# Causal attention and a two-branch MoE in one kernel: MoE steps drawn from the first entry whose tokens are there, and shares that count all ready work

## The chip, the cores and the metric

The kernel runs on one core of a Trainium2 chip. Its time is the device time of one execution in microseconds: the median of three runs was 264.66 us (264.55 to 265.04). The profile is of one further execution, which is recorded as 265.55 us; the span from its first to its last instruction is 263.7 us, at a granted TensorE clock of 0.998.

The engines are named as in the profile: PE (TensorE, with PEld for its weight loads), DVE (VectorE), ACT (ScalarE), POOL (GpSimd) and SP (the queue that issues most of the DMAs).

## What is computed

Block-causal attention over 8 batches and 8 heads, 576 tokens of 64 dimensions, followed by a feed-forward layer over all 4608 tokens, with `d_model` 512 and `d_ff` 1024:

```
scores = q @ k.T / 8, kept where query block (64 tokens) >= key block
x      = softmax(scores) @ v, heads side by side   # (4608, 512)
g      = maximum(x @ w1, x @ w2)                   # (4608, 1024)
out    = g @ w_out                                 # (4608, 512)
```

The kernel uses max(h1, h2) = max(h1 - h2, 0) + h2. With d = w1 - w2 and M = w2 @ w_out it computes `out = x @ M + max(x @ d, 0) @ w_out`. So there is one wide product h = x @ d per token, and y adds 4 matmuls against M to 8 against w_out.

## The kernel before

**Attention.** Heads go in pairs (`NPAIR` = 32, a pair's number is p) and pairs in groups of two (`NG` = 16, a group's number is g); two groups make a batch. For a pair, three tiles of scores are made in PSUM (`tile_0`, `tile_1`, `tile_2`), ACT takes their exponentials to `aT` (L391, and a corner at L447), POOL sets masked parts to zero (L396), and two pairs later (`LAG` = 2) `av` multiplies with v (L475). DVE divides by the sum of each row and writes `xp` (L481, L482). The score tiles have two PSUM buffers of two banks each, used by nothing else.

**From xp to xT.** The MoE needs x with features on partitions, as `xT`. For the groups of the first two batches and for the last group `x_out` transposes on PE and copies with DVE or ACT (L513 to L519). For groups 4 to 14 the SP queue transposes by DMA (`x_dma`, L493) after the attention of a group's last pair; for them `x_out` only notes that the tokens of a batch are there. That note is `done_tokens`.

**MoE.** Tokens are cut into ten spans: 256 and 320 of the first batch, then 512 each from token 576 on, the last 448. Spans are not aligned with batches of 576. `h_unit(i, f)` makes one of 8 tiles of h of span i: 4 matmuls, then max with zero by DVE into `g` (L220). With its first tile POOL copies the rows that the last span left over (`carry`, L207). `y_unit(i, s)` makes 128 rows of the output: 12 matmuls into one bank (L257), a copy by ACT (by DVE for the first two spans), and a store by SP (L262, L263). `bT_unit` and `m_unit` make M, at the start. All of these, `av`, the transposes and the warming matmuls share four PSUM banks (`ps_m`). `g` has two buffers.

**The order of the work.** The kernel fixes the order of each engine's instructions itself (`manual_schedule`): instructions stand as they are written. The units are generators that give control back after each matmul. `plan` lists them: for every span h(i, 0) to h(i, 7), and from span 3 on the tiles y(i-1, s) between them. Each entry has the number of tokens that must be there (`need`), a cost per step (1.0 for 512 columns) and its number of steps. `fill(n)` takes steps worth n in that order. It stops where the entry at hand needs tokens that are not there, though a later one may have them: y of span 2 needs 1088 tokens, and stands in the list between tiles of h of span 3, which needs 1600.

**The groups.** The first two groups are written out by hand (L572 to L666), then groups 2 (L667 to L678) and 3 to 15 (L680 to L701). `fill_of(g)` gives the steps of a group: what is `ready`, less 6, over the groups that are left until the next batch is there; the last group takes 45. A group takes them in five fills: `hi` before the first half of each pair's attention, `lo` between its halves, and the rest at the group's end. After the last group come two attentions with fills between them, the last transposes (L709), and all the work that is left (L710).

Of the kernel before, what the change touches and what calls it, by code (L numbers as in the profile page):

```python
# [14 lines left out]
def kernel(  # L15
# [20 lines left out]
    NFF = d_ff // P  # L36
    NTOK = B * S
# [109 lines left out]
    for j in range(d_ff // WB):  # L147
        row, n = (1, j) if j < 3 else (3, 0)
# [50 lines left out]
    done_tokens = [0]  # L199
# [82 lines left out]
    units = []  # L282
    NY = NDM + NFF

    def plan():
        def h(i, f):
            t0, w = spans[i]
            units.append((h_unit(i, f), t0 + w, w / SPAN, NDM))

        def y(i, s, last=False):  # L290
            t0, w = spans[i]
            if last:
                units.append((y_last(i, s), t0 + w, 0.333, 3 * NY))
            else:
                units.append((y_unit(i, s), t0 + w, 1.0, NY))

        for i in range(NSPAN):
            for f in range(NFF):
                h(i, f)
                if i == 0 and f % 2:  # L300
                    units.append((bT_unit(f // 2), 0, 0.25, 2 * NDM))
                if i > 2 and f % 2 == 0 and f // 2 < tiles[i - 1]:
                    y(i - 1, f // 2)
            if i == 1:
                for n in range(2 * NDM):
                    units.append((m_unit(n // NDM, n % NDM), 0, 0.5, NFF))
                for j in range(2):
                    for s in range(tiles[j]):
                        y(j, s)
        n = tiles[-1]  # L310
        for s in range(n):
            y(NSPAN - 1, s, s == n - 1)

    plan()
    steps = [(u, need, cost) for u, need, cost, n in units for _ in range(n)]
    at = [0]


    def ready():
        n, total = at[0], 0.0  # L320
        while n < len(steps) and steps[n][1] <= done_tokens[0]:
            total += steps[n][2]
            n += 1
        return int(total)

    def fill(n):
        while n > 0 and at[0] < len(steps) and steps[at[0]][1] <= done_tokens[0]:
            u, _, cost = steps[at[0]]
            next(u)
            n -= cost  # L330
            at[0] += 1


    def warm_up(n):
# [38 lines left out]
    def pad_keys(p):  # L373
        nc.gpsimd.tensor_copy(
            out=kz_r[p % NT].rearrange("p (a c) -> p a c", c=BLK)[:, 0:3:2],
            in_=kT_r[p % NT][:, S - 3 * BLK:].rearrange("p (a c) -> p a c", c=BLK)[:, 0:3:2],
        )
# [50 lines left out]
    def tile_0(p):  # L428
        u = ps_s.tile([P, 2, 512], FP32, name="ps_s", tag="s")
        scores(p, u, 0, 0, 0, 512)  # L430
        return lambda: (exp(p, u, 512, 0), mask(p, 0))

    def tile_1(p):
        u = ps_s.tile([P, 2, 512], FP32, name="ps_s", tag="s")
        scores(p, u, 0, 0, 512, 64)
        scores(p, u, 64, 1, 128, 448)
        return lambda: (exp(p, u, 512, 512), mask(p, 576))

    def tile_2(p):
        u = ps_s.tile([P, 2, 512], FP32, name="ps_s", tag="s")  # L440
        corner_scores(p, u, 320)
        scores(p, u, 0, 2, 256, 320)
        scores(p, u, 384, 3, 448, P)

        def out():
            exp(p, u, 512, 1024)
            nc.scalar.activation(  # L447
                out=aT_r[p % NA][BLK:, :, 1536:AW], in_=u[BLK:, :, 320:320 + BLK],
                func=AF.Exp, scale=scale,
            )  # L450
            mask(p, 1024)
            mask(p, 1344)
        return out

    def region(*tiles):
        for out in tiles:
            out()
# [29 lines left out]
    def x_by_dma(g):  # L487
        return BY_DMA <= g < NG - 1

    def x_dma(g):  # L490
        b, u = divmod(g, GPB)
        for s in range(2):
            nc.sync.dma_start_transpose(  # L493
                out=xT[:, 2 * u + s, b * S:b * S + NCH * P].rearrange(
                    "p (t w) -> p t w", w=P),
                in_=xps[g][:, s].rearrange("p t a d -> p (t a d)"),
            )

    def x_out(g, t0=0, t1=NCH, copies=(dve, dve)):
        b, u = divmod(g, GPB)  # L500
        if x_by_dma(g):
            if u == GPB - 1:
                done_tokens[0] = (b + 1) * S
            return
        xp = xps[g]
        n = t1 - t0
        n_odd = min(t1, NCH - 1) - t0
        pe = ps_m.tile([P, 2, n, BLK], BF16, name="ps_xe", tag="m")
        po = ps_m.tile([P, 2, n_odd, BLK], BF16, name="ps_xo", tag="m")
        for s in range(2):  # L510
            for t in range(t0, t1):
                src = xp[:, s, t].rearrange("p a d -> p (a d)")
                nc.tensor.transpose(pe[:, s, t - t0, :], src[:BLK], ident[:BLK, :BLK])  # L513
                if t < NCH - 1:
                    nc.tensor.transpose(po[:, s, t - t0, :], src[BLK:], ident[BLK:, BLK:])
        dst = xT[:, 2 * u:2 * u + 2, b * S + t0 * P:b * S + t1 * P].rearrange(
            "p s (t h w) -> p s t h w", h=2, w=BLK)
        copies[0](out=dst[:, :, :, 0], in_=pe[:])
        copies[1](out=dst[:, :, :n_odd, 1], in_=po[:])  # L519
        if u == GPB - 1:  # L520
            done_tokens[0] = min(b * S + t1 * P, (b + 1) * S)
# [8 lines left out]
    def fill_of(g):  # L530
        if g == NG - 1:
            return 45
        left = 5 - g if g < 5 else 2 - (g - 5) % 2
        return -(-max(0, ready() - KEEP) // left)


    def pool_work(s):
        g, i = divmod(s, 2)
        if s == 4:
            load_qk(4, (SP, SP), gated=True)  # L540
        elif s == 5:
            load_qk(5, (SP, SP), gated=True)
            cast("q", 4, ((pool, 0, RPP),))
            cast("k", 4, ((pool, 0, RPP),))
        else:
            if i == 1 and g + 3 < NG:
                load_qk(g + 3, (SP, SP), gated=True)
            if i == 1 and g + 2 < NG:
                cast("q", g + 2, ((pool, 0, RPP),))
                cast("k", g + 2, ((pool, 0, RPP),))  # L550
            nb, j = divmod(s + 2, HP)
            if nb < B:
                for c in ((0, 1), (2, 3), (4,), ())[j]:
                    load_v(nb, c)
# [4 lines left out]
    def t_pair(s):  # L559
        outs = [transposes(nm, g, (dve, act)) for nm, g in T_AT.get(s, [])]  # L560
        return lambda: [f() for f in outs]
# [5 lines left out]
    def av_with(p, n):  # L567
        av(p, [0, 1])
        fill(n)
        av(p, [2, 3, 4])  # L570
# [55 lines left out]
    masks_q(1)  # L626
    load_w(3)
    fill(4)
    burst_q1(2)
    transposes("q", 2, (dve, act))()  # L630
# [18 lines left out]
    load_qk(3, (SP, SP), gated=True)  # L649
    x_out(0, 2, NCH)  # L650
    fill(2)
    diff_w(1)
    outs = tile_0(4), tile_1(4)
# [15 lines left out]
    n = fill_of(GPB)  # L669
# [9 lines left out]

    for g in range(GPB + 1, NG):  # L680
        a, b = 2 * g, 2 * g + 1
        if x_due:
            x_out(x_due.pop())
        n = fill_of(g)
        region(tile_0(a), tile_1(a))
        lo, hi = max(3, n // 18), n * 2 // 9
        for p, tiles in ((a, lambda: (tile_2(a), tile_0(b))), (b, lambda: (tile_1(b), tile_2(b)))):
            fill(hi)
            av_with(p - LAG, lo)
            if p % 2 and x_by_dma(g - 1):  # L690
                x_dma(g - 1)
            copy_out = t_pair(p)
            outs = tiles()
            copy_out()
            region(*outs)
            if p % 2 and g + 1 < NG:
                pad_keys(p + 1)
                pad_keys(p + 2)
            pool_work(p)
        x_due.append(g - 1)  # L700
        fill(n - 2 * (lo + hi))  # L701
    for p in range(NPAIR - LAG, NPAIR):
        if x_due:
            x_out(x_due.pop())
        av_with(p, 5)
        if p % 2 and x_by_dma(p // 2):
            x_dma(p // 2)
        fill(9)
    x_out(NG - 1)  # L709
    fill(len(steps))  # L710

# [33 lines left out]
```

The softmax here doesn't subtract the row's maximum and nothing guards it: scores larger than these inputs give would overflow.

## Time and profile before

| engine | busy us | share of the span | instructions |
|---|---|---|---|
| PE, matmuls | 250.0 | 95% | 2983 |
| PEld, weight loads | 139.6 | 53% | 2983 |
| DVE | 137.2 | 52% | 301 |
| ACT | 140.9 | 53% | 198 |
| POOL | 109.9 | 42% | 274 |

How to read the views. A line of a timeline has start, duration, engine, line of the kernel, operation, output and inputs, the count, and in brackets the idle time of the engine just before it and what ended that. A line of waits has the waiting engine and line, then whom it waited for, then the sum in us, the number of times and the longest. A table of stretches has, for each stretch, its length and then the busy time of PE, PEld, DVE, ACT and POOL with the number of instructions in brackets, the granted clock, the mean share of the DMA engines and GB/s. [...]

The groups are found in PE's timeline by their first score matmuls: group 5 begins at 67.93 us, group 8 at 100.26, group 9 at 113.32. For groups 6 and 7 the point is taken where PE came to these matmuls, 75.85 and 85.05 us; both then waited 0.32 us. The last transposes of xp on PE begin at 213.13 us.

### The profile page before, as it was taken

The numbers are of one execution on the slowest core, as the hardware profiler recorded it, in microseconds if no ns is written. First come the engines' busy times: TensorE is split into PE (matmuls) and PEld (weight loads), VectorE is DVE, ScalarE is ACT, GpSimd is POOL, SyncE is SP. The second block draws the span as 40 slices with busy tenths as digits, with TensorE's granted clock in tenths as the row PEclk, the third lists the DMA queues.
The fourth block names the chain that finished last, engine by engine and source line by source line (L and its number), as shares of the span: only waits on it lengthen the run. The fifth ranks groups of instructions, "written<-read, shape, count | busy, mean of one in ns | idle before, by whom it ended". The sixth has DMA issues, their size and how long they took to land.

```text
span 263.7 us, 7204 instructions
## 1 busy us (share of the span) xinstructions
PE 250.0 (95%) x2983; PEld 139.6 (53%) x2983; DVE 137.2 (52%) x301; ACT 140.9 (53%) x198; POOL 109.9 (42%) x274
## 2 busy tenths in 40 slices
PE   8698799999989799999999999999999999999995
PEld 2346566856546455555555555555555544444444
DVE  4867996656668554545454545454544452323200
ACT  2788552676797484848575757575755100111111
POOL 2987914484577647254635563456311000000000
PEclk9999999999999999999999999999999999999999
DMA  7999996689599949986997599679613411112122
GB/s 247 314 218 298 188 234 158 247 94 252 144 182 256 234 68 264 132 252 71 262 150 232 81 227 178 227 82 126 106 42 81 52 66 57 63 58 82 40 95 104
DMA packets 71265, 41.30 MB, mean 157 GB/s; under 512 B 53568, under 2 KB 58048, under 8 KB 71232
## 3 DMA queue, kind: packets, MB, share of 16 engines
q1 hardware_dynamic: 28544, 31.27, 43.2%
q0 software_dynamic: 42272, 8.92, 38.1%
q10 hardware_dynamic: 416, 0.66, 0.7%
q8 instruction: 23, 0.38, 0.6%
q14 instruction: 10, 0.08, 0.1%
HBM read 34.60 MB, written 9.44 MB: 167 GB/s over the span
## 4 chain that ended last, share of the span: by engine, by line
PE 85%; DMA 5%; POOL 3%; ACT 2%; DVE 2%; issue 1%; ACTq 0%; POOLq 0%
PE ps_y L257 35%; PE ps_h L215 21%; PE ps_o L475 10%; PE ps_s L367 7%; PE ps_w L337 3%; DMA qraw<-in_q_dram 3%; PE ps_M L238 3%; PE ps_qT L348 2%; ACT aT L391 2%; DMA xT<-xp 2%; PE ps_kT L348 2%; POOL vv L136 1%; PE ps_y L272 1%; PE ps_s L385 1%; POOL wo_sb L168 1%
## 5 line engine op out<-in xcount | busy, mean ns | idle before, releaser
L391 ACT ACTIVATE aT<-ps_s 128x1024 bf16<-128x1024 f32 (+2 forms) x100 | 95.9, 996 | 28.9 <-PE ps_s L367 26.9
L220 DVE TENSOR_SCALAR g<-ps_h 128x512 bf16<-128x512 f32 (+3 forms) x80 | 50.7, 636 | 63.9 <-PE ps_h L215 62.9
L215 PE MATMUL ps_h<-xT,d_sb 128*128 128x512 bf16 (+3 forms) x320 | 71.7, 358 | 1.8 <-DVE d_sb L162 1.2
L257 PE MATMUL ps_y<-wo_sb,g 128*128 128x512 bf16 x280 | 69.9, 379 | 0.0
L396 POOL MEMSET aT<- 64x128 bf16 x124 | 22.3, 200 | 78.7 <-ACT aT L391 78.0
L475 PEld LDWEIGHTS <-aT 128*128 128x128 bf16 x960 | 37.2, 98 | 14.0 <-issue 2.1
L215 PEld LDWEIGHTS <-d_sb 128*128 128x128 bf16 x320 | 28.7, 98 | 29.7 <-issue 3.5
L262 ACT COPY y<-ps_y 128x512 f32<-128x512 f32 x31 | 18.2, 588 | 48.5 <-PE ps_y L257 45.6
L257 PEld LDWEIGHTS <-g 128*128 128x128 bf16 x280 | 25.7, 98 | 30.0 <-issue 2.6
L475 PE MATMUL ps_o<-vv,aT 128*128 128x65 bf16 x960 | 39.7, 194 | 0.0
L257 PE MATMUL ps_y<-m_sb,xT 128*128 128x512 bf16 x140 | 37.9, 380 | 0.0
L367 PE MATMUL ps_s<-qT,kT 64*128 64x64 bf16 (+6 forms) x344 | 31.4, 280 | 3.9 <-ACT aT L447 1.6
L136 POOL DMA_DIRECT2D vv<-in_v_dram x40 | 33.7, 848 | 1.6 <-issue 1.2
L482 DVE TENSOR_TENSOR xp<-ps_o,rec 128x256 bf16<-128x256 f32 (+1 forms) x64 | 31.4, 491 | 2.2
L481 DVE RECIPROCAL rec<-ps_o 128x4 f32<-128x4 f32 (+1 forms) x64 | 12.1, 189 | 35.4 <-PE ps_o L475 34.9
L356 ACT COPY qT<-ps_qT 128x576 bf16<-128x576 bf16 (+1 forms) x17 | 10.3, 614 | 24.8 <-PE ps_qT L348 24.8
L257 PEld LDWEIGHTS <-xT 128*128 128x128 bf16 x140 | 12.9, 98 | 16.0 <-issue 3.0
L132 POOL CAST qn<-qraw 128x1152 bf16<-128x1152 f32 (+1 forms) x16 | 16.9, 1058 | 8.6 <-DMA qraw<-in_q_dram 8.6
L367 PEld LDWEIGHTS <-kT 64*128 64x128 bf16 x344 | 12.3, 94 | 13.7 <-issue 8.2
L207 POOL COPY g<-g 128x512 bf16<-128x512 bf16 x8 | 4.9, 613 | 31.5 <-DVE g L220 30.9
L132 POOL CAST kn<-kraw 128x1152 bf16<-128x1152 f32 (+1 forms) x15 | 17.1, 1139 | 1.1 <-DMA kraw<-in_k_dram 1.0
L356 ACT COPY kT<-ps_kT 128x576 bf16<-128x576 bf16 x15 | 9.6, 639 | 10.5 <-PE ps_kT L348 10.0
(57 smaller groups left out, 161.8 us busy)
## 6 DMA issues: line engine op xcount, KB each, us to landing
qraw<-in_q_dram SPq DMA_DIRECT2D x16, 576.0 KB, 4.8
out_dram<-y SPq DMA_DIRECT2D x35, 256.0 KB, 2.6
kraw<-in_k_dram SPq DMA_DIRECT2D x15, 576.0 KB, 6.0
vv<-in_v_dram POOLq DMA_DIRECT2D x32, 128.0 KB, 6.0
w1raw<-in_moe_w_dram POOLq DMA_DIRECT2D x4, 512.0 KB, 7.8
xT<-in_moe_w_dram POOLq DMA_DIRECT2D x4, 256.0 KB, 8.5
wo_sb<-in_moe_w_out_dram POOLq DMA_DIRECT2D x2, 512.0 KB, 8.1
kraw<-in_k_dram ACTq DMA_DIRECT2D x1, 576.0 KB, 5.6
```

The lines of the kernel that those rows point to most:

```text
L132: copy(out=n[:, j0:j1], in_=t[:, j0:j1])
L136: nc.gpsimd.dma_start(out=vv_r[b % NV][P - rows:, c, :, :D], in_=v[b, :, c * P:c * P + rows, :].rearrange("h p d -> p h d"),)
L215: nc.tensor.matmul(pt[:, :w], d_sb[:, c, f * P:(f + 1) * P], xT[:, c, t0:t0 + w], start=(c == 0), stop=(c == NDM - 1),)
L220: nc.vector.tensor_scalar_max(g[:, f, m:m + w], pt[:, :w], 0.0)
L257: nc.tensor.matmul(py[:], lhs, rhs, start=(n == 0), stop=(n == len(terms) - 1),)
L262: (dve if i < 2 else act)(out=y[:], in_=py[:])
L356: (copy or copies[i])(out=t[:, p0 * RPP:p1 * RPP].rearrange("q (p j) -> q p j", j=RPP), in_=pts[i][:, :, p0:p1].rearrange("q j p -> q p j"),)
L367: nc.tensor.matmul(ps[:, hh, col:col + w], kT[r, k0:k0 + P], qT[r, q0:q0 + w], start=True, stop=True,)
L391: nc.scalar.activation(out=aT_r[p % NA][:, :, a0:a0 + w], in_=ps[:, :, :w], func=AF.Exp, scale=scale,)
L396: (eng or nc.gpsimd).memset(aT_r[p % NA][BLK:, :, a0:a0 + BLK], 0.0)
L475: nc.tensor.matmul(po[:, gi, hh, :], a[:, hh, a0:a0 + P], vv[:, c, h0 + 2 * hh, :], start=(mm == 0), stop=(mm == n_mm - 1),)
L482: nc.vector.tensor_mul(xp[:, :, ts[0]:ts[0] + n, p % 2].rearrange("q s t d -> q t s d"), po[:, :, :, :D], rec[:, :n].to_broadcast([P, n, 2 ...
```

## The change

The list of steps becomes a list of units, `todo`, with one unit in hand, `current`. `fill` finishes the unit in hand, and then takes the first one in the list whose tokens are there, whatever stands before it. It returns what it could not spend. `ready` adds up all units whose tokens are there. In groups whose newest tokens come by DMA, the first fill sees the tokens of before first, and what it can't spend so goes to the new ones. At the end, 12 steps of old work stand after the last transposes before the new tokens count.

```diff
-    steps = [(u, need, cost) for u, need, cost, n in units for _ in range(n)]
-    at = [0]
+    todo = [[n, u, need, cost] for u, need, cost, n in units]
+    current = []
     def ready():
-        n, total = at[0], 0.0
-        while n < len(steps) and steps[n][1] <= done_tokens[0]:
-            total += steps[n][2]
-            n += 1
-        return int(total)
+        return int(sum(n * cost for n, _, need, cost in current + todo if need <= done_tokens[0]))
     def fill(n):
-        while n > 0 and at[0] < len(steps) and steps[at[0]][1] <= done_tokens[0]:
-            u, _, cost = steps[at[0]]
-            next(u)
-            n -= cost
-            at[0] += 1
+        while n > 0:
+            if not current:
+                k = next((k for k, t in enumerate(todo) if t[2] <= done_tokens[0]), None)
+                if k is None:
+                    return max(0, n)
+                current.append(todo.pop(k))
+            t = current[0]
+            next(t[1])
+            n -= t[3]
+            t[0] -= 1
+            if not t[0]:
+                current.pop()
+        return 0
...
     for g in range(GPB + 1, NG):
         a, b = 2 * g, 2 * g + 1
+        old = done_tokens[0]
         if x_due:
             x_out(x_due.pop())
-        n = fill_of(g)
+        n, new = fill_of(g), done_tokens[0]
...
-            fill(hi)
+            if p == a and x_by_dma(g - 2):
+                done_tokens[0] = old
+            rest = fill(hi)
+            done_tokens[0] = new
+            fill(rest)
             av_with(p - LAG, lo)
...
+    old = done_tokens[0]
     x_out(NG - 1)
-    fill(len(steps))
+    done_tokens[0] = old
+    fill(NY)
+    done_tokens[0] = NTOK
+    fill(len(units) * NFF * 12)
```

## The prediction

> **What bounds the kernel now.** I read the page first (shares, slices), then the waits of TensorE in two stretches, then PE's timeline group by group, and last the DMA transposes.
>
> ```profile
> PE 250.0 (95%) x2983; PEld 139.6 (53%) x2983; DVE 137.2 (52%) x301; ACT 140.9 (53%) x198; POOL 109.9 (42%) x274
> PE   8698799999989799999999999999999999999995
> PE 85%; DMA 5%; POOL 3%; ACT 2%; DVE 2%; issue 1%; ACTq 0%; POOLq 0%
> ```
>
> TensorE is the bound: 95% of the span, 85% of the chain that ended last. It is not full everywhere: after the opening, slices 12 and 13 (6.6 us each, so 72.5 to 85.7 us) fall to 8 and 7. The waits of TensorE between 66 and 92 us:
>
> ```profile
> PE ps_s L367 <- ACT aT L447: 1.6, 2, 0.8
> PE ps_s L367 <- DVE g L220: 0.6, 2, 0.3
> PE ps_h L215 <- DMA xT<-xp: 0.5, 1, 0.5
> ```
>
> The same question from 92 us to the end lists no wait at all. So from there only the number of matmuls counts, and a matmul moved forward out of that stretch shortens it by a whole matmul. Busy times by stretch, cut at the first score matmul of groups 5, 6, 7 (the third only to its q transposes), then everything after, then two later groups (8 and 9):
>
> ```profile
> core 0: us, PE busy (x) PEld busy (x) DVE busy (x) ACT busy (x) POOL busy (x), PEclk, DMA share, GB/s
> 67.93:75.85 7.92, 7.92 (x154) 4.94 (x147) 6.48 (x15) 6.10 (x8) 4.66 (x13) 1.00 0.71 217
> 75.85:85.05 9.20, 8.06 (x140) 4.86 (x141) 6.38 (x15) 7.56 (x11) 7.59 (x19) 1.00 1.47 219
> 85.05:91.20 6.15, 4.43 (x50) 2.33 (x49) 2.90 (x6) 3.40 (x5) 4.28 (x12) 1.00 1.38 187
> 91.20:260.60 169.40, 169.40 (x1752) 89.17 (x1749) 74.21 (x152) 82.56 (x118) 52.95 (x138) 1.00 0.66 126
> 100.26:113.32 13.06, 13.06 (x167) 7.07 (x166) 6.65 (x14) 8.62 (x12) 6.59 (x18) 1.00 1.18 186
> 113.32:126.37 13.05, 13.05 (x166) 7.04 (x166) 6.67 (x14) 8.62 (x12) 6.63 (x18) 1.00 0.87 173
> ```
>
> To be seen: group 6 lasts 9.20 us with PE busy 8.06; the start of group 7 lasts 6.15 with 4.43; later groups last 13.05 without a gap. ACT is busy 7.56 of 9.20 us in group 6, so there the exponentials set the pace. PE's timeline shows where it stands:
>
> ```profile
> 76.17 0.39 PE L367 MATMUL ps_s<-qT,kT 64*128 64x512 bf16 x2 [0.32 <-DVE g L220]
> 77.39 0.39 PE L367 MATMUL ps_s<-qT,kT 64*128 64x64 bf16 x4 [0.82 <-ACT aT L447]
> ...
> 85.37 0.39 PE L367 MATMUL ps_s<-qT,kT 64*128 64x512 bf16 x2 [0.32 <-DVE g L220]
> 86.59 0.40 PE L367 MATMUL ps_s<-qT,kT 64*128 64x64 bf16 x4 [0.82 <-ACT aT L447]
> 86.91 1.90 PE L215 MATMUL ps_h<-xT,d_sb 128*128 128x512 bf16 x8
> 88.65 0.34 PE L475 MATMUL ps_o<-vv,aT 128*128 128x65 bf16 x6
> 89.46 0.86 PE L215 MATMUL ps_h<-xT,d_sb 128*128 128x512 bf16 x2 [0.47 <-DMA xT<-xp]
> ```
>
> A group's first scores come before the exponentials of the last group's tiles have left the two score buffers, and h of span 3 comes before its tokens are transposed. Both happen because these groups carry too little MoE work in between.
>
> **What the Trainium skill says.** "TensorE: Matmul & The Clock Gate", section "Wait — 56ns, not 53.3ns?", gives 215.7 ns from start to start for 512 columns. The trace agrees; the chain that ended last has
>
> ```profile
> 202.09 2.59 PE ps_y L257 x12
> ```
>
> which is 215.8 ns each, while the rows of such matmuls show 379 ns, because they overlap. I cost a matmul at 0.2158, not at its row. "Perfetto Trace Analysis", section "Tensor Engine Instruction (MATMUL, LD_WEIGHTS)", says that the end of a matmul is an estimate. That agrees too: the gaps listed are shorter than the time lost (below). "DMA: Bandwidth & Descriptors", section "Issuing engines are not separate DMA queues", says that transfers from all engines interleave on the same 16. Here one transpose took 3.1 to 7.0 us to land, depending on what else was under way.
>
> **The change, part by part.** The unit of account is one `fill` step, one matmul of 512 columns. I followed `fill`, `ready` and `fill_of` through the span list (256, 320, eight spans from token 576, the last of 448).
>
> 1. *Up to the end of group 4: nothing.* No work is passed over there; the counts and their order are the same (32, 31 and 30 steps for groups 2 to 4).
>
> 2. *Shares of groups 5 and 6.* With 1152 tokens there, the old count stops at the first h of span 3 (needs 1600): 38 ready, so (38-6)/2 = 16 steps for each group. The new count adds y of span 2 (needs 1088), 4x12 = 48 steps: 86 ready, 40 steps each, all of which it finds. So 2x24 = 48 matmuls move from the tail (245 steps after the last attention in the old, 12+185 = 197 in the new) into groups 5 and 6. From group 7 on both have 40 a group, and 45 in the last.
>
> 3. *What they cost in groups 5 and 6.* A full group lasts 13.055 us (mean of the two rows above) with 40 steps: 40x0.2158 = 8.63, so 4.42 us are scores, transposes and attention. A group with 16 steps would last 4.42+3.45 = 7.87 without a wait. Measured: group 5 7.92 (0.05 over), group 6 9.20 (1.33 over), start of group 7 6.15 against 3.99 in groups 8 and 9 (100.26 to 104.25; 113.32 to 117.31): 2.16 over. Together 3.54 us lost. The gaps recorded make (9.20-8.06)+(6.15-4.43) = 2.86; as ends are estimates, I take 3.54 and keep 2.86 as the lower end.
>
> 4. *What takes the place of the waits.* With 18 steps (3.9 us) before the next group's scores, in place of 4 (0.86 us), the last exponentials (1.95+0.27 us) are out, as they are in groups 8 to 14. The transposes of group 6 land 5.3 us after issue; h of span 3 reaches them 15.5 us after the group's first score (115.78-100.26), the issue is at 9.2 (109.41-100.26), so 1.1 us are to spare. Then all 3.54 us go.
>
> 5. *h of span 2 starts in the first fill of group 5*, after six y matmuls. Its tokens come from DVE copies that end at 69.0 us (68.18+0.49, then 0.41), and PE gets there at 68.5+6x0.2158 = 69.8. No wait.
>
> 6. *Order in the later groups.* Old: every group finishes 4 h and 2 y tiles. New: odd groups finish 8 h and 1 y, even groups 3 y. DVE in odd groups: 6.65+4x0.69 = 9.4 of 13.06 us; ACT in even groups: 8.62+0.59 = 9.2. Both stay under PE. Inside a run of h a tile takes PE 0.86 us and DVE 0.69. The tightest reuses of the four shared PSUM banks, by the built order: y's bank taken by q's transposes 0.99 us after y's last matmul (ACT starts about 0.2 later and takes 0.59); and y's bank of an odd group's first fill taken by attention at 3.1 us after the group's start, while ACT, behind two exponentials, frees it at 2.9 (103.16-100.26). The old order has its own reuse at 0.99 us, h by DVE, in nine places and shows no wait. I take zero, and keep 0.1 us in ten groups, 1 us, as the upper end.
>
> 7. *POOL's copy of g's carry (0.61 us) and g's two buffers.* The copy is issued with h's first step as before, but the h that it reads has been done for a whole group, not for a moment; POOL, behind it masks and casts, can only gain. y of the span before is complete when h starts, so no buffer is missing. Zero, hidden under PE.
>
> 8. *SP.* The y stores move: an even group's third y is now ready at about 12.4 us into the group, when the two transposes are issued (9.2 to 12.5) and the next q and k loads stand ahead of it in the queue. It starts as the transposes land (114.4 to 115.2 in group 8). Zero; up to 0.7 us at each of five boundaries kept for the rival.
>
> 9. *Tokens withheld in the first fill of odd groups.* h of the new span comes after 6 old steps before and after (h before, y now). Zero. In the tail too h of span 8 comes 13 matmuls after the last transposes in both. Zero.
>
> Sum: -3.54 us on a traced span of 263.7, that is 260.2; that execution counts as 265.55 in the times. On the median of 264.66: **261.1 us**.
>
> **Rivals.**
> - *A: part is given back.* The new order waits where a bank, ACT or a transpose is just late (items 6 and 8): 1 us from banks, or 0.5 us at three boundaries. Against it: no wait at all in 169 us of the same machinery. Gain 1.5 to 2.8: 262.5 us.
> - *B: slower, by late transposes.* If even groups, now with one store more, saw the landing of the most crowded group (issue at 148.57 us: 7.0 and 6.1 us), the second transpose would land at 10.5+6.1 = 16.6 us, and h needs it at 15.7 (the fourth h step). 0.87 us at the starts of groups 7, 9, 11, 13 and 15 make 4.4: 261.1+4.4 = 265.5 us. It decides against the change from 0.71 us each (3.54/5). Against it: that was an odd group, with four v loads; even groups have one, and landed in 3.0 to 5.3.
> - *C: nothing moves.* A tail as long as before would need TensorE waiting in the tail by 10.4 us (48x0.2158) or in groups 5 and 6 as much; it is excluded for the tail, where every y evacuation (0.59) hides under 2.59 us of matmuls. Waits of half a microsecond in each of seven groups give 264.6 us.
>
> **How the numbers follow.** Main case 0.78, its own range 260.6 to 261.9 (lower end: 0.5 us more, from small gaps that the rows hide; upper: the recorded 2.86). A 0.13, B 0.05, C 0.04. A change under 0.2% (0.5 us) can't be told from none. Faster: main and A, 0.91; same: C, 0.04; slower: B, 0.05. The range 260.3 to 262.7 takes in the main case and A's likelier part.
>
> **What would show it.** Right: groups 5 and 6 last about 13 us each; TensorE has no wait on ACT's L447 form or on a transpose from group 5 on; group 7's first score comes about 9.0 us later (26.1 for 17.1), and from it to the end is about 12.5 us less (10.36 of matmuls and 2.16 of waits). Wrong: new waits of attention or q transposes for ACT's y copy, h waiting for transposed tokens at the start of odd groups, or groups over 13.1 us.

## The result, and the profile after

| | time, us | against before |
|---|---|---|
| before | 264.68 median (264.55 to 265.04, 4 runs) | 1 |
| changed | 261.19 median (260.83 to 261.69, 4 runs) | 0.9867, 95% interval 0.9847 to 0.9887 |
| changed, again, in a later set | 261.20 median (260.65 to 261.56, 6 runs) | 0.9843 (0.9819 to 0.9867) |

261.1 us was predicted, from a median before of 264.66. In the later set the kernel before has a median of 265.09 us. Ratios and intervals, here and below, leave out two runs in a slower state of the chip, one of the kernel before (268.08 us, granted clock 0.987) and one of experiment 7 (269.04 us, 0.986).

The page of the changed kernel's profile, its first line and PE's row of slices (now 6.5 us each):

```profile
PE 244.8 (94%) x2949; PEld 139.4 (54%) x2983; DVE 137.6 (53%) x301; ACT 141.3 (55%) x198; POOL 109.8 (42%) x274
PE   8688799999999999999999999999999999999995
```

The two slices with 8 and 7 are gone; the slices under 9 that are left are the first five, ahead of the change, and the last one, as before. The count of matmuls is 2949 for 2983 weight loads: 34 records are missing in this trace. That matters for the waits of TensorE from 66 to 260 us, where the list has only these:

```profile
PE ps_h L215 <- issue: 1.0, 6, 0.2
PE ps_y L257 <- issue: 0.8, 5, 0.2
```

They wait for nothing that the profile shows, and those that I followed in the timeline stand where a fill shows one matmul less than it issues (7 where 8 are). In the trace of the second run of the same kernel this view lists nothing at all. The waits for `aT`, for DVE and for a DMA transpose are gone. Groups 5 to 8, in the table of stretches (length, then busy time of PE, PEld, DVE, ACT, POOL):

```profile
67.41:80.44 13.03, 12.77 (x175) 7.17 (x171) 10.31 (x21) 7.55 (x10) 7.59 (x22) 1.00 0.85 168
80.44:93.44 13.00, 12.79 (x165) 7.08 (x166) 4.42 (x11) 9.31 (x13) 6.59 (x18) 1.00 1.08 191
93.44:106.43 12.99, 12.78 (x163) 7.08 (x166) 8.87 (x18) 8.03 (x11) 6.62 (x18) 1.00 0.99 168
106.43:119.42 12.99, 12.78 (x163) 7.07 (x165) 4.41 (x11) 9.31 (x13) 6.57 (x18) 1.00 1.01 195
```

To be seen: groups 5 and 6 now last as long as the later ones. DVE carries the odd groups (busy 10.31 and 8.87 us) and ACT the even ones (9.31); neither gets near 13. PE's timeline has the scores of groups 6 and 7, and h of span 3, at once:

```profile
80.44 0.61 PE L371 MATMUL ps_s<-qT,kT 64*128 64x512 bf16 x6
93.44 0.61 PE L371 MATMUL ps_s<-qT,kT 64*128 64x512 bf16 x6
...
95.28 0.59 PE L215 MATMUL ps_h<-xT,d_sb 128*128 128x512 bf16 x2
95.89 0.81 PE L215 MATMUL ps_h<-xT,d_sb 128*128 128x512 bf16 x3
```

The brackets with idle time that stood on the same matmuls before are missing. The two traces by stretch, cut at the same points as in the prediction (group 15 starts at 191.65 us before and 197.53 after):

| stretch | before | after | difference | predicted |
|---|---|---|---|---|
| start to group 5 | 67.93 | 67.41 | -0.52 | 0 |
| groups 5 and 6 | 17.12 | 26.03 | +8.91 | +9.0 |
| group 7 | 15.21 | 12.99 | -2.22 | -2.16 |
| groups 8 to 14 | 91.39 | 91.10 | -0.29 | 0 |
| group 15 to the end | 72.05 | 61.67 | -10.38 | -10.36 |
| span | 263.7 | 259.2 | -4.5 | -3.54 |

The first row is not the change: up to there the program is the same, and in the traces of the experiments group 5 starts anywhere from 67.25 to 68.14 us. The rest is -3.98 us, 0.44 more than predicted. Of this, 0.29 us lie in groups 8 to 14, where I had set zero. Those groups do not all last the same: five take 12.99 or 13.00 us, group 9 takes 13.02 and group 10 13.11, where before each took 13.05 or 13.06. Group 10 holds a wait that is new:

```profile
132.44:145.55 13.11, 12.90 (x164) 7.16 (x166) 4.42 (x11) 9.31 (x13) 6.60 (x18) 1.00 1.07 191
134.90 0.60 PE L257 MATMUL ps_y<-wo_sb,g 128*128 128x512 bf16 x2
135.86 0.59 ACT L262 COPY y<-ps_y 128x512 f32<-128x512 f32 x1 [0.98 <-ACT aT L395]
136.37 0.55 PE L352 MATMUL ps_qT<-ident,qn 64*128 64x64 bf16 x18
```

The last matmul of y starts at 135.12, ACT copies its bank from 135.86 to 136.45, and of the 18 transposes of q the first starts at 136.37 and the second, which waits for ACT, only at 136.50. In group 8 ACT starts its copy 0.46 us after the start of y's last matmul, here 0.74, and there the first two transposes start within 0.01 us of each other. So q's transposes wait 0.12 us for y's bank, without a bracket in the timeline. The second trace of the same kernel and that of experiment 6 have it too (group 10 lasts 13.11 and 13.10 us). Why ACT starts later in this one group is open.

The experiments ask two things: where the 0.06 us in most of these groups comes from, and, the larger question, whether the reason for the 3.5 us is the right one.

The theory: TensorE lost 3.5 us because groups 5 and 6 had too few steps between a group's last exponentials and the next group's scores; 48 steps brought forward from a tail without gaps fill that time. The rivals: the order of drawing as such, the holding back of new tokens, or merely the place where the steps stand inside a group.

### The profile page after: what moved, and what is told of

Read it like the earlier page. It is cut to its first block, busy times and chain, and to the rows that moved or that the text cites. A ratio compares the mean times of both kernels' runs of the same rounds, so it can differ in the third digit from the quotient of the medians.

```text
span 259.2 us, 7161 instructions
## 1 busy us (share of the span) xinstructions
PE 244.8 (94%) x2949; PEld 139.4 (54%) x2983; DVE 137.6 (53%) x301; ACT 141.3 (55%) x198; POOL 109.8 (42%) x274
## 4 chain that ended last, share of the span: by engine, by line
PE 85%; DMA 5%; POOL 3%; issue 2%; ACT 2%; DVE 1%; POOLq 0%; ACTq 0%
PE ps_y L257 35%; PE ps_h L215 22%; PE ps_o L479 10%; PE ps_s L371 8%; DMA qraw<-in_q_dram 5%; PE ps_M L238 3%; PE ps_qT L352 2%; PE ps_kT L352 2%; POOL vv L136 1%; ACT aT L395 1%; PE ps_y L272 1%; DVE qn L132 1%; PE ps_w L341 1%; PE ps_s L389 1%; POOL wo_sb L168 1%
## 5 line engine op out<-in xcount | busy, mean ns | idle before, releaser
L215 PE MATMUL ps_h<-xT,d_sb 128*128 128x512 bf16 (+3 forms) x306 | 67.4, 357 | 2.7 <-DVE d_sb L162 1.2
L257 PE MATMUL ps_y<-wo_sb,g 128*128 128x512 bf16 x275 | 69.1, 379 | 0.4 <-issue 0.3
L257 PE MATMUL ps_y<-m_sb,xT 128*128 128x512 bf16 x128 | 36.5, 380 | 1.2 <-issue 0.8
L257 PEld LDWEIGHTS <-xT 128*128 128x128 bf16 x140 | 12.2, 98 | 15.1 <-issue 3.5
```

Source lines behind the costliest of these rows:

```text
L215: nc.tensor.matmul(pt[:, :w], d_sb[:, c, f * P:(f + 1) * P], xT[:, c, t0:t0 + w], start=(c == 0), stop=(c == NDM - 1),)
L257: nc.tensor.matmul(py[:], lhs, rhs, start=(n == 0), stop=(n == len(terms) - 1),)
```

## The experiments

**1. The order alone.** The changed kernel, with the old way of counting:

```diff
-        return int(sum(n * cost for n, _, need, cost in current + todo if need <= done_tokens[0]))
+        total = 0.0
+        for n, _, need, cost in current + todo:
+            if need > done_tokens[0]:
+                break
+            total += n * cost
+        return int(total)
```

> The new order of drawing with the old counting: ready stops at the first entry in the list whose tokens are not there, so groups 5 and 6 get 16 steps again, not 40. Theory (the gain is the 48 matmuls that the shares move): the waits of the score matmuls at the start of groups 6 and 7 are back, about 1.3 us each; only the wait for the DMA transpose at the start of group 7 is gone (0.65 us), since y of span 2 now stands ahead of h of span 3. 264.0 us (263.5 to 264.6). Rival (the gain comes from the order itself, fewer hand-overs between h and y): 261.2 to 262.5 us.

Measured 264.0 us, as expected, ratio 0.9972 (0.9960 to 0.9983). Waits of TensorE from 66 to 260 us in its trace:

```profile
PE ps_s L376 <- ACT aT L456: 1.6, 2, 0.8
PE ps_s L376 <- DVE g L220: 0.6, 2, 0.3
```

These are the two score waits of the kernel before, to the tenth; the wait for the transpose is gone. The order is worth 0.3%, the shares the other 1.0 to 1.3%. From the first score of group 5 to that of group 15 this trace takes 122.64 us, against 123.72 before: 1.08 less. Of this, 0.90 us lie in group 7, and the rest in groups 9, 11 and 13, which last 12.99 us.

**2. The slack by itself.** The kernel before, with matmuls of zeros in the two groups and nothing moved:

```diff
             fill(hi)
+            if g in (5, 6):
+                warm_up(5)
...
         fill(n - 2 * (lo + hi))
+        if g in (5, 6):
+            warm_up(14)
```

> The kernel before with 24 more matmuls of zeros, 512 columns, in each of groups 5 and 6 (5 after each hi fill, 14 at the group's end), whose results nothing reads; no MoE work is moved. It prices the slack alone. Theory: 48 x 0.2158 = 10.36 us of matmuls, of which 3.5 us lie in waits that vanish: 264.7 + 6.8 = 271.5 us (271.0 to 272.2). Rival (the slack is only the recorded 2.86 us): 272.2. Rival (no slack, the gain of the change came from elsewhere): 275.0 us.

Measured 271.97 us against 264.87, ratio 1.0268 (1.0243 to 1.0292). So 10.36 us of matmuls cost 7.1 us (6.4 to 7.7 by the interval), and 3.3 us (2.6 to 3.9) of them lay in waits. That interval holds both 3.54 and 2.86, so the time alone can't choose between the two; it does exclude "no slack" (275.0 us). The trace is sharper. Its score matmuls of groups 6 and 8:

```profile
80.42 0.61 PE L367 MATMUL ps_s<-qT,kT 64*128 64x512 bf16 x6
...
106.41 0.61 PE L367 MATMUL ps_s<-qT,kT 64*128 64x512 bf16 x6
```

From group 5 (67.39) to group 8 are 39.02 us, against 32.33 before: 6.69 more for 10.36 us of matmuls, so 3.67 us lay in waits, by one trace against one. Its trace lists no wait of TensorE after 66 us. The recorded idle time alone (2.86) is below what the trace has.

**3. Half of the steps.** The tail gives up 48 steps as in the changed kernel, but only 24 of them go to groups 5 and 6. The count of ready work then hands the other 24 to groups 7 and 8, which take 52 steps each.

```diff
+        if g in (5, 6):
+            return 28
         left = 5 - g if g < 5 else 2 - (g - 5) % 2
```

> The changed kernel with the shares of groups 5 and 6 fixed at 28 steps, not 40: half of the 48 matmuls are moved into them, the others go to groups 7 and 8, which have no wait to fill. Theory (steps pay only until the waits are filled; 10 steps, 2.16 us, now stand between the last tiles of a group and the next scores, against 2.2 us of exponentials): nearly the whole gain, 261.2 to 261.9 us, with at most 0.4 us of waits at the start of groups 6 and 7. Rival (gain in proportion to the steps moved): 262.9 us.

Measured 261.54 us, ratio 0.9877 (0.9855 to 0.9900): 24 steps in groups 5 and 6 bring practically what 48 bring. Groups 5 and 6 last 10.44 and 10.50 us, within 0.05 of 4.42 us of other work plus 28 x 0.2158, and the only wait in the list is another one, in group 7:

```profile
PE ps_h L215 <- ACT y L262: 0.2, 1, 0.2
```

Group 7 lasts 16.04 us, 0.40 more than 4.42 plus 52 x 0.2158; that is about what this run is slower than the changed kernel. A step pays only while a wait is left to fill. After that it costs in the group what it saves in the tail. The table of stretches can't say where that point is; this run shows that 28 steps are enough, and none was made between 16 and 28.

**4. The small remainder.** The kernel before, with one engine changed for the copies of y:

```diff
-                (dve if i < 2 else act)(out=y[:], in_=py[:])
+                dve(out=y[:], in_=py[:])
```

> The kernel before with all copies of y out of PSUM made by DVE, not ACT. It tests a small second source: groups 8 to 14 last 13.055 us before and 12.99 after, and in the trace of before the first matmul of a y tile starts 0.08 us late, just after ACT, behind two exponentials, has freed a bank. Theory (that bank wait is the 0.06 us): groups 8 to 14 fall to about 12.99 us, 264.2 us in all. Rival (the 0.06 us is the price of more hand-overs between h and y): 13.055 us as before and 264.7 us.

Measured 264.58 us, ratio 0.9991 (0.9978 to 1.0004): no difference in the time that these runs can tell, where 264.2 us was expected. The interval holds a gain of 0.4 us as well as none, so the time decides nothing. The groups say which theory holds. In PE's timeline of this kernel the scores of groups 8 and 9 start at

```profile
100.32 0.61 PE L367 MATMUL ps_s<-qT,kT 64*128 64x512 bf16 x6
113.32 0.61 PE L367 MATMUL ps_s<-qT,kT 64*128 64x512 bf16 x6
```

and every group from 8 to 14 lasts 12.99 to 13.01 us, where before it was 13.055, with every hand-over between h and y in its place. So the 0.06 us was y's bank, freed late by ACT. In the timeline of before, the matmul that then waited, and the ACT copy that freed its bank:

```profile
102.71 0.60 PE L215 MATMUL ps_h<-xT,d_sb 128*128 128x512 bf16 x2
103.22 0.38 PE L257 MATMUL ps_y<-m_sb,xT 128*128 128x512 bf16 x1
...
102.57 0.59 ACT L262 COPY y<-ps_y 128x512 f32<-128x512 f32 x1
```

Two steps from 102.71 end at 103.14; the next starts at 103.22, just after 103.16. No idle time is written beside it, because the row of the matmul before still covers it. With DVE's copies the same matmul follows at once (two steps from 102.78, the next at 103.21). In the one execution that was traced (265.12 us, a slower one of this kernel), the gain of these groups was lost in group 7, where the wait for the transpose is 1.3 us and not 0.5:

```profile
PE ps_h L215 <- DMA xT<-xp: 1.3, 2, 1.1
```

Whether DVE's copies make that wait longer is open. They are not needed for it: in the next experiment, where ACT copies, the same wait is 1.3 us too. The transposes meant took 4.5 and 5.3 us to land in the trace of before, 5.2 and 6.0 here.

**5. Full groups, but the later ones go short.** The kernel before, old `fill`, with span 2's y tiles listed right after its h tiles, so that groups 5 and 6 take 40 steps:

```diff
-                if i > 2 and f % 2 == 0 and f // 2 < tiles[i - 1]:
+                if i > 3 and f % 2 == 0 and f // 2 < tiles[i - 1]:
                     y(i - 1, f // 2)
+            if i == 2:
+                for s in range(tiles[2]):
+                    y(2, s)
```

> The kernel before, old fill and old counting, with one edit to the list: y of span 2 stands right after h of span 2, so groups 5 and 6 find 86 steps and take 40 each, as in the changed kernel. Later y tiles stay between tiles of the next h, out of reach, so groups 7 and 8 now find 38 and take 16 each. Theory (the step that counts is that work in reach never runs short again, not the fuller groups 5 and 6 alone): the waits turn up two groups later, at the starts of groups 8 and 9, about 3.5 us in all, and the time is that of before, 264.3 to 265.2 us. Rival (full groups 5 and 6 are enough, later groups have slack of their own): 261.2 to 262.0 us.

Measured 265.13 us against 265.09, ratio 0.9998 (0.9983 to 1.0012). All the idle time of TensorE from 66 to 125 us in its timeline:

```profile
101.87 0.39 PE L370 MATMUL ps_s<-qT,kT 64*128 64x512 bf16 x2 [0.32 <-DVE g L220]
103.08 0.39 PE L370 MATMUL ps_s<-qT,kT 64*128 64x64 bf16 x4 [0.82 <-ACT aT L450]
111.07 0.39 PE L370 MATMUL ps_s<-qT,kT 64*128 64x512 bf16 x2 [0.32 <-DVE g L220]
112.28 0.40 PE L370 MATMUL ps_s<-qT,kT 64*128 64x64 bf16 x4 [0.82 <-ACT aT L450]
115.20 0.38 PE L215 MATMUL ps_h<-xT,d_sb 128*128 128x512 bf16 x1 [0.50 <-DMA xT<-xp]
116.41 0.38 PE L215 MATMUL ps_h<-xT,d_sb 128*128 128x512 bf16 x1 [0.83 <-DMA xT<-xp]
```

The same score waits with the same lengths, two groups later (group 8 comes to its scores at 101.5 us, group 9 at 110.8), and a wait for transposes that is longer (1.33 us for 0.47). Groups 5 and 6 are full and nothing is gained. The rule "first entry whose tokens are there" matters because it keeps every later y in reach, not because it fills these two groups.

**6. No tokens held back.**

```diff
-            if p == a and x_by_dma(g - 2):
-                done_tokens[0] = old
-            rest = fill(hi)
-            done_tokens[0] = new
-            fill(rest)
+            fill(hi)
...
-    done_tokens[0] = old
-    fill(NY)
-    done_tokens[0] = NTOK
```

> The changed kernel without holding back new tokens: no old tokens in the first fill of odd groups, and after the last transposes no 12 steps of old work. In the groups this alters nothing, since six steps of y in hand come first anyway. In the tail h of span 8 comes after 1 step, 0.2 us, while its tokens leave PSUM by DVE about 1.3 us after the first transpose. Theory: one new wait of 0.7 us in the tail, 261.9 us. Rival (the holding back of tokens is part of the gain in the groups, by sparing waits for DMA transposes): 263 us or more. Rival (DVE is early enough): 261.2 us.

The edit leaves the order of matmuls in the groups as it is, since there six steps of y in hand come first with it and without it. Only the tail differs.

Measured 261.29 us, ratio 0.9859 (0.9835 to 0.9883), with 261.20 for the changed kernel in the same set: no difference. The only wait that the list has, after 66 us, with the copy that ended it:

```profile
219.53 0.59 PE L215 MATMUL ps_h<-xT,d_sb 128*128 128x512 bf16 x2
219.82 0.41 DVE L523 COPY xT<-ps_xo 128x512 bf16<-128x512 bf16 x1
220.29 2.54 PE L215 MATMUL ps_h<-xT,d_sb 128*128 128x512 bf16 x11 [0.16 <-DVE xT L523]
```

I expected 0.7 us. The first two h matmuls read the rows of group 14, which were there long before; only the third reads the last group's. From 219.53 two steps end at 219.96, and the third starts at 220.29: 0.33 us. Holding tokens back costs nothing and is worth no more than that here.

**7. The same 16 steps in another place.** The kernel before, groups 5 and 6 with 12 steps at the end and 1 in each earlier fill:

```diff
         lo, hi = max(3, n // 18), n * 2 // 9
+        if g in (5, 6):
+            lo, hi = 1, 1
```

> The kernel before with the 16 steps of groups 5 and 6 kept, but 12 of them at the group's end and 1 in each earlier fill. It asks if the waits at the starts of groups 6 and 7 come of where the steps stand or of how many there are. Theory (too few steps: ACT needs 7.6 us of exponentials and copies in a group of 7.9 us of PE work, so a wait taken away at one place comes back at another): the waits at the group starts vanish and new ones of about 0.5 to 1 us stand inside the groups, before the second pair of tiles; 264.0 to 265.2 us. Rival (placement alone): 262.0 to 263.0 us.

Measured 265.59 us, ratio 1.0017 (0.9995 to 1.0039): no gain, and 0.4 us above the range that I expected (264.0 to 265.2). All the idle time of TensorE from 66 to 125 us in its timeline:

```profile
72.83 0.23 PE L385 MATMUL ps_s<-qT,kz 64*128 64x64 bf16 x4 [0.58 <-ACT aT L391]
81.38 0.23 PE L385 MATMUL ps_s<-qT,kz 64*128 64x64 bf16 x4 [0.46 <-ACT aT L391]
88.45 0.83 PE L215 MATMUL ps_h<-xT,d_sb 128*128 128x512 bf16 x2 [1.39 <-DMA xT<-xp]
```

The waits at the group starts are gone, and shorter ones for the same exponentials stand inside the groups. Together they are 1.0 us, less than half of the 2.2 before, so the place does count for these waits. But the transposes landed 6.4 and 7.2 us after issue in this trace, against 4.5 and 5.3 before, and h waited 1.4 us for them. From group 5 to group 8 the trace takes 31.93 us for 32.33. Whether the new places made the transposes late is open. By the time of 13 runs, placement alone gains nothing.

## Why the prediction was right

**The sum.** The table above agrees with its three terms to 0.1 us each. The step that carried it was to count the lost time from start to start (3.54 us) and not by recorded idle time (2.86): the group starts of filler show 3.67. That the time came within 0.1 us of 261.1 is in part luck. The first set has the kernels 3.5 us apart, the later set 3.9 by its medians, and the traces 4.0 without the opening. The 3.54 us also rests on one trace, and its wait for a transpose is 0.5 us there and 1.3 us in the trace of y_by_dve.

**Items 2 and 3, the shares.** Shown: without them (order_only) the score waits are back; with half of them in groups 5 and 6 (share28) nearly all is gained; with the same steps and no gain in the tail (filler) the slack is what was counted.

**Item 4, what replaces the waits.** Shown for groups 5 to 8 in the table of stretches. That the y tiles must stay in reach for the groups after 6 was used in item 2 ("from group 7 on both have 40") without being named as the condition; y2_listed_early shows that the whole gain hangs on it.

**Item 6, the order in the later groups.** Set at zero with up to 1 us of loss kept; it gained about 0.06 us in five groups and 0.03 in group 9, and lost 0.05 us in group 10. The error was the step from "the list shows no wait" to "only the number of matmuls counts". The list has none, but the starts had one of 0.08 us. Of the tight reuses that the prediction named, y's bank by q's transposes did wait in one group: ACT started its copy 0.52 us after y's last matmul was through (135.12 + 0.2158), and not the 0.2 reckoned with. So two of the prediction's signs of being wrong, q's transposes waiting for ACT's y copy and a group over 13.1 us (13.11), did appear, at 0.12 us in one place and not at 0.1 us in ten.

**Items 8 and 9, SP and the tokens.** Rival B's late transposes did not come: in the changed kernel's trace those issued in groups 6, 8, 10, 12 and 14 land 2.6 to 3.8 us after issue, and no h waits. The prediction gave 3.1 to 7.0 us for one transpose and put the spread down to the other traffic; the trace of before has 2.6 to 7.0, and no run isolates what decides it. Item 9 holds: in the tail 13 steps were more than was needed.

**Rivals.** A (part given back), B (slower) and C (no gain) are refuted by the time; what A feared did happen, but for 0.12 us. The order as the source of the gain, raised for the experiments, holds for 0.3% of the 1.3 to 1.6%, mostly the wait for one transpose.

**Left open.** Why the first 67 us vary by up to 0.9 us from trace to trace (the granted clock does not order them: 68.14 us at 1.000, 67.39 at 0.998); what decides when a transpose lands; and why ACT is late in group 10.

## What to carry to other kernels

Where one engine has no gap in a late stretch and gaps in an early one, work brought forward is worth the gaps that it fills and no more: measure them from start to start, and try half the dose. Before filling a short stretch, follow the scheduler's counts to the end, since work that is only taken from the next stretch moves the wait there. A list walked strictly in order stops at the first entry that isn't ready, so its own count of ready work can be far too low while later entries are free.

## What the runs showed of the hardware

A list of idle time can miss waits on TensorE altogether: the row of a matmul of 512 columns lasts 379 ns while its successor can start after 215.8, so here a wait shorter than 0.16 us leaves no gap, and a longer one shows that much less. The 0.08 us of y's bank before and the 0.12 us of q's transposes after stand in no list. Over groups 5 to 7 the recorded 2.86 us stood for 3.5 to 3.7.

A DMA transpose of 128 x 640 bf16 within SBUF landed 2.6 to 7.0 us after issue in the traces of before and after, and up to 7.2 us in that of late_steps. In the changed kernel one landed after 2.7 us in group 6 and another after 5.3 us in group 7. A plan in which work must meet such a transpose to the tenth of a microsecond has no ground here.
